# A banded attention and two MLPs in one planned kernel: the first MLP's tiles in blocks of 3, 4, 4, 4 and 3, a shorter warm-up and new priorities

## The chip, the cores and the metric

The kernel runs on one core of a Trainium2 chip. The metric is the device time of one execution in microseconds (us), given as the median of several runs.

## The reference

The input is q, k and v for 4 batches of 8 heads, 576 positions and 64 columns each. A causal attention within a window of 128 positions with a linear bias is followed by a first MLP with a rational activation and a second with SiLU; all is in float32.

```python
scores = scale * q @ k.T                      # per batch and head
scores = where((rel >= 0) & (rel < 128), scores - slope[h] * abs(rel), -1e9)
attn = softmax(scores); x = attn @ v          # -> x: 2304 tokens x 512
h = x @ w_in                                  # 512 x 2048
g = (a0 + a1*h + a2*h*h + a3*h**3) / (1 + |b0|*|h| + |b1|*h*h + 1e-6)
x = g @ w_out                                 # 2048 x 512
h = x @ w2_in;  g = h / (1 + exp(-h));  return g @ w2_out
```

The 2304 tokens are 18 tiles of 128.

## The kernel before

Every product of the MLPs is made of three products on numbers split into a high and a low part (xh and xl, gh and gl, and the two halves of a weight), so each has its elementwise work: a cast and a subtraction. The weights arrive as 64-bit numbers; ACT (L561, L564), DVE (L567), and ACT or POOL (L466, L474, L485) turn them into the two halves.

The first MLP works on blocks of tiles. `blk1` gives their sizes (4, 4, 3, 4 and 3). For each block and each of 16 slices f of the hidden layer, `step` issues 12 products into a bank `h` (L889 to L891; two banks in turn), a chain of five ACT and six DVE instructions for the rational function (L905 to L934), a cast and a subtraction that make gh and gl, and 12 products into four accumulators (L958 to L960). Each instruction works on the whole block at once, so on 512 columns for four tiles and 384 for three. Blocks 0 and 1 are taken in two parts each: f 0 to 9 of block 0, f 0 to 9 of block 1, then f 10 to 15 of both; partial sums go by way of DRAM. The first pass over a slice prepares its weights, and writes the first matrix's halves to a scratch (L597), from which later blocks read them (L606). Block 0 is therefore the one that pays for the weights.

Ahead of a block, `group` does its attention for four pairs of heads: scores (L698), masking and a minimum on DVE (L704, L711), the exponential on ACT (L715), the normalization on POOL (L734), a transposition (L754), masked copies (L785 to L803), the product with v (L831), and xh and xl (L846 to L855). Block 0's attention is done before its first step; block 1's beside block 0's f 0 to 9; block 2's only when block 0 is through, since x has two buffers.

The second MLP takes the 18 tiles in three groups of six by a scheme with seven products in place of eight. Sums of its weights are prepared on the way (`prep`, L1122) as filler work, written to DRAM, and streamed in (L1133).

The order of all this is made by a planner at build time. Each operation has a priority in units of steps, a cost, and one or more engines that may take it (for instance `'whi': 'act|pool'`); `schedule` simulates the engines and gives a free engine the ready operation of the best priority (`look` is how much later a better one may be). The constants in `OPT` and the list `SHIFTS` (first operation, count, shift) move priorities. The order that comes out is the order in each engine's queue; nothing is reordered on the chip. DMA issues nearly all lie in SP's queue. Before the first step, planned PE gaps of over 300 ns are filled with products on an identity whose result nobody uses (`spin`, L511): `warm` of them at the start, then `fill` (0.6) of each gap. A float32 product makes two records in the profile.

Of the kernel before, what the change touches and what calls it, by code (L numbers as in the profile page):

```python
# [30 lines left out]


OPT = {
    'blk1': '4,4,3,4,3',
    'res': 0,
    'lag': 2,
    'gh': 'act|pool',
# [13 lines left out]
    'tabs': 'pool',  # L51
    'stb': 3,
    'strb': 3,
    'wpro': 0.256,
    'dS': -1.52,
    'dT': 0.037,
    'dA': 0.149,
    'dm': 0.366,
    'look': 0.451,
    'pw': -0.72,  # L60
    'pwo': -0.374,
    'dg': -5.616,
    'lead': 2.536,
    'slk': 0,
    'warm': 6,
    'fill': 0.6,
    'fillmin': 300.0,
    'fs': 10,
    'ob': 3,
    'pl': -0.721,  # L70
    'vlead': -1.233,
    'qlead': -1.974,
    'keen': 9999.0,
    'norm0': 'pool',
    'sq': 'act',
# [4 lines left out]
    'mk02': 'dd',  # L80
    'mk03': 'dd',
    'xl00': 'd',
    'xl01': 'd',
    'xl02': 'p',
    'xl03': 'd',
    'alt': 0,
    'gh0': 'act|dve',
    'gl0': 'pool',
    'la': 8.921,
    'lb': 302.617,  # L90
    'dm2': 1.231,
    'sums': 'pool',
    'fhi': 'act|pool',
    'flo': 'dve|pool',
# [5 lines left out]
    'tsum': 'pool',  # L100
    'th': 'act|dve',
    'tl': 'dve|pool',
    'tlead': 1.016,
    'hlead': -0.505,
    'oq': 'sp',
    'pw2': 511.696,
    'rw2': 25.851,
    'pwo2': 1331.915,
    'rwo2': 14.569,
    'xlead': -0.854,  # L110
    'slead': 0.691,
    'shift': 'act',
    'tail': 1,
}
# [1 line left out]


SHIFTS = [
# [6 lines left out]
]  # L125


# [31 lines left out]
LAG = {"kd": 1400.0, "qd": 1400.0, "vh": 1400.0, "wraw": 1200.0, "ws": 400.0, "wv": 400.0, "tab": 0.0}  # L159
# [12 lines left out]
class Plan:  # L172
# [11 lines left out]
    def op(self, prio, eng, cost, fn, reads=(), writes=(), after=(), dma=False):  # L184

        o = Op()
        o.eng, o.cost, o.fn, o.prio, o.idx = eng, cost, fn, prio, len(self.ops)
        o.alts = eng if isinstance(eng, dict) else {eng: (cost, fn)}

        o.banks = {t[:2] for t in list(reads) + list(writes) if t[0] in ("h", "atA", "atB") or t[0].startswith("acc")}  # L190
        o.port = {e for e in o.alts if e == "pool" or e == "dve" and not o.banks}
        o.deps, o.allocs = set(after), []
        o.dma = dma or eng == "sp"
        o.lag = max([LAG.get(t[0], 0.0) for t in writes], default=0.0) if o.dma else 0.0
        for t in list(reads) + list(writes):
            key, reg = t[:2], t[2:]
            if key not in self.tile_ops:
                self.tile_ops[key] = []
                o.allocs.append(key)
            else:  # L200
                o.deps.add(self.tile_ops[key][0])
            self.tile_ops[key].append(o)
        for t in reads:
            key, reg = t[:2], t[2:]
            for w, r in self.writers.get(key, ()):
                if not reg or not r or r == reg:
                    o.deps.add(w)
        for t in writes:
            key, reg = t[:2], t[2:]
            for w, r in self.writers.get(key, ()):  # L210
                if not reg or not r or r == reg:
                    o.deps.add(w)
            for w, r in self.readers.get(key, ()):
                if not reg or not r or r == reg:
                    o.deps.add(w)
        for t in reads:
            self.readers.setdefault(t[:2], []).append((o, t[2:]))
        for t in writes:
            self.writers.setdefault(t[:2], []).append((o, t[2:]))
        o.deps.discard(o)  # L220
        self.ops.append(o)
        return o
# [166 lines left out]
def plan_kernel(ctx, tc, qn, kn, vp, table, w1, wo1, w2, wo2, out):  # L389
    nc = tc.nc if tc is not None else None  # L390
# [3 lines left out]
    RES, LAG = OPT["res"], OPT["lag"]  # L394
    pl = Plan()
# [64 lines left out]
    def do_copy(engs, n, make, psum=False, scale=None):  # L460

        sc = 1.0 if scale is None else scale

        def on_act():
            o, i = make()
            nc.scalar.activation(out=o, in_=i, func=AF.Copy, scale=sc) if scale is not None else nc.scalar.copy(o, i)  # L466

        def on_dve():
            o, i = make()
            nc.vector.tensor_scalar(out=o, in0=i, scalar1=sc, scalar2=None, op0=ALU.mult) if scale is not None else nc.vector.tensor_copy(o, i)  # L470

        def on_pool():
            o, i = make()
            nc.gpsimd.tensor_scalar(out=o, in0=i, scalar1=sc, scalar2=1.0, op0=ALU.mult, op1=ALU.mult)  # L474

        return any_of(engs, {"act": (c_act(n, psum), on_act), "dve": (c_dve(n) if psum else c_dve2x(n), on_dve), "pool": (c_pool_ts(n), on_pool)})

    def do_tt(engs, n, op, make):
        def on_dve():
            o, a, b = make()  # L480
            nc.vector.tensor_tensor(out=o, in0=a, in1=b, op=op)  # L481

        def on_pool():
            o, a, b = make()
            nc.gpsimd.tensor_tensor(out=o, in0=a, in1=b, op=op)  # L485

        return any_of(engs, {"dve": (c_dve(n), on_dve), "pool": (c_pool_tt(n), on_pool)})


    if tc is not None:  # L490
        nc.scalar.preload_act_table_set("natural_log_exp_and_others")
        tab_all = tab_p.tile([P, 6 * P + 16], F32, name="tab")
        tab = tab_all[:, :6 * P].rearrange("p (t c) -> p t c", c=P)
        coef = tab_all[:, 6 * P:]
        ident = const.tile([P, P], F32, name="ident")
# [18 lines left out]
        T[("h", "spin")] = h_p.tile([P, 512], F32, tag="h", name="spin")  # L514
        spin(OPT["warm"])

    pl.op(-98, "pe", 427 * OPT["warm"], first_spin, reads=[("ident", 0)], writes=[("h", "spin")])
    pl.spin = spin

    late = []  # L520

    def late_consts():
        for part, cols in ((0, slice(0, 3 * P)), (1, slice(3 * P, 6 * P + 16))):
            pl.op(-91.0 + 0.5 * part, "sp", 700, lambda cols=cols: nc.sync.dma_start(tab_all[:, cols], table[:, cols]), writes=[("tab", part)])
        for part in range(2):
            for h in range(H):
                pl.op(-70 + 0.1 * h + 10 * (h // 2) + 25 * part, do_copy("act" if h + part == 0 else OPT["tabs"], 2 * P,
                      lambda h=h, part=part: (tabs[:, h, 2 * part:2 * part + 2], tab[:, 4 * part:4 * part + 2]), scale=-8.0 * 2.0 ** -(h + 1)), 0, None,
                      reads=[("tab", part)], writes=[("tabs", h, part)])
        late.append(("na", 0))  # L530
        late.append(("ab", 0))
        pl.op(-3, "dve", 80, lambda: nc.vector.tensor_scalar(out=na, in0=coef[:, 0:4], scalar1=-1.0, scalar2=None, op0=ALU.mult),
              reads=[("tab", 1)], writes=[("na", 0)])
        pl.op(-3, "act", 200, lambda: nc.scalar.activation(out=ab, in_=coef[:, 4:6], func=AF.Abs), reads=[("tab", 1)], writes=[("ab", 0)])
# [457 lines left out]
    lead = OPT["lead"]  # L992
# [12 lines left out]

    att_load(0, -92, slot[0] + slot_w[0] - OPT["vlead"])
    late_consts()
    for gi in range(len(groups) - 1):
        att_load(gi + 1, slot[gi] - 0.25 * slot_w[gi] - OPT["qlead"], slot[gi + 1] + slot_w[gi + 1] - OPT["vlead"])
# [12 lines left out]
    for f in range(KF):  # L1022
        p = pos[0, f] + OPT["pw"]
# [4 lines left out]
        p = pos[0, f] + LAG + 0.5 + OPT["pwo"]  # L1028
# [431 lines left out]
```

## Time and profile before

| | |
|---|---|
| median of 3 runs | 869.03 us (868.75 to 869.29) |
| the profiled execution | 869.16 us; its span 867.3 us |
| PE busy | 855.2 us (99%), 5076 products |
| DVE, ACT, POOL busy | 643.1, 603.1, 637.9 us (74%, 70%, 74%) |
| granted TensorE clock | 1.00 in every stretch |
| DMA | 228.94 MB, 264 GB/s over the span |

The time of the profiled execution is 1.86 us longer than its span; the rest lies around the first and last instruction. PE's busy time counts the products on the identity too. The attention of block 0 and the first steps lie in the first 58 us, the rest of block 0's f 0 to 9 up to some 115 us, its f 10 to 15 near 175 to 200 us, and the second MLP from about 475 us to the end.

### The profile page before, as it was taken

Reading aid. Unit: us, or ns where it says so; the run is one execution under the profiler, and the core shown is the slowest. Engines: PE = TensorE matmul, PEld = TensorE weight load, DVE = VectorE, ACT = ScalarE, POOL = GpSimd, SP = SyncE. Lnnn points to the kernel's source line nnn. Section 1 sums busy time; section 2 is a strip of 40 time slices with the busy share of each in tenths; the row PEclk is TensorE's granted clock in tenths of the full one; section 3 lists DMA queues with packets and bytes.
Section 4 is the critical chain, followed back from the end, with each engine's and each line's share of the span. In section 5 each row is a group of like instructions: output and inputs, shape, how many; then the busy total and the mean of one; then the engine's idle time right before and its main releaser. Section 6 shows DMA issues by size and latency. Waiting matters only on the chain.

```text
span 867.3 us, 15300 instructions
## 1 busy us (share of the span) xinstructions
PE 855.2 (99%) x5076; PEld 765.1 (88%) x5076; DVE 643.1 (74%) x1308; ACT 603.1 (70%) x1291; POOL 637.9 (74%) x613
## 2 busy tenths in 40 slices
PE   8989999999999999999999999999999999999998
PEld 6667778877788998777889999999999999999998
DVE  7899897789999898998889984357733477433652
ACT  6699997799888988887889984446434365344452
POOL 4778845666888897878899677479954599744884
PEclk9999999999999999999999999999999999999999
DMA  7746764586889887876797889898888888878884
GB/s 253 264 161 214 243 223 137 169 277 227 289 310 321 294 280 263 306 255 238 275 349 240 295 297 356 262 318 281 281 277 250 292 288 282 295 248 258 252 269 169
DMA packets 80462, 228.94 MB, mean 264 GB/s; under 512 B 8192, under 2 KB 17152, under 8 KB 80384
## 3 DMA queue, kind: packets, MB, share of 16 engines
q1 hardware_dynamic: 78080, 219.59, 76.2%
q10 hardware_dynamic: 2304, 8.39, 2.4%
q8 instruction: 40, 0.66, 0.3%
q14 instruction: 38, 0.31, 0.1%
HBM read 178.66 MB, written 49.28 MB: 263 GB/s over the span
## 4 chain that ended last, share of the span: by engine, by line
PE 82%; DVE 5%; ACT 4%; POOL 3%; DMA 3%; issue 2%; SPq 0%; ACTq 0%; POOLq 0%; DVEq 0%
PE acc L958 6%; PE h L889 6%; PE acc L960 6%; PE acc L959 6%; PE h L891 5%; PE h L890 5%; PE z_a L1233 4%; PE z_b L1300 4%; PE z_a L1234 4%; PE z_a L1235 4%; PE z_b L1301 4%; PE z_b L1299 4%; PE bank_atA L831 3%; PE bank_atA L698 2%; PE bank_atA L1233 1%
## 5 line engine op out<-in xcount | busy, mean ns | idle before, releaser
L485 POOL TENSOR_TENSOR xl_b<-g,xh_b 128x384 fp32r<-128x384 f32 x81 | 90.6, 1119 | 69.6 <-ACT xh_b L466 67.8
L466 ACT CAST xh_b<-g 128x384 fp32r<-128x384 f32 x162 | 83.0, 514 | 64.3 <-PE z_b L1301 42.0
L958 PE MATMUL acc<-gh,wo 128*128 128x512 f32 (+1 forms) x320 | 121.1, 378 | 0.0
L960 PE MATMUL acc<-gl,wo 128*128 128x512 f32 (+1 forms) x320 | 118.7, 371 | 0.1
L959 PE MATMUL acc<-gh,wo 128*128 128x512 f32 (+1 forms) x320 | 117.8, 368 | 0.0
L481 DVE TENSOR_TENSOR xl_b<-g,xh_b 128x384 fp32r<-128x384 f32 x87 | 87.3, 1014 | 30.3 <-ACT xh_b L466 29.1
L485 POOL TENSOR_TENSOR gl<-t,gh 128x512 fp32r<-128x512 f32 (+1 forms) x76 | 93.0, 1224 | 15.9 <-ACT gh L466 12.5
L385 ACT ACTIVATE g<-t_a 128x384 f32<-128x384 f32 x72 | 37.9, 526 | 75.2 <-DVE t_a L378 75.2
L485 POOL TENSOR_TENSOR g<-g,g 128x384 f32<-128x384 f32 x72 | 84.5, 1185 | 2.0
L889 PE MATMUL h<-xh,ws 128*128 128x512 f32 (+1 forms) x224 | 84.2, 376 | 0.4 <-DVE t L934 0.4
L891 PE MATMUL h<-xh,ws 128*128 128x512 f32 (+1 forms) x224 | 82.2, 367 | 0.0
L890 PE MATMUL h<-xl,ws 128*128 128x512 f32 (+1 forms) x224 | 82.1, 367 | 0.0
L958 PEld LDWEIGHTS acc<-gh,wo 128*128 128x128 f32 x320 | 60.1, 188 | 13.4 <-issue 5.6
L960 PEld LDWEIGHTS acc<-gl,wo 128*128 128x128 f32 x320 | 60.0, 188 | 9.5 <-POOL gl L485 1.5
L959 PEld LDWEIGHTS acc<-gh,wo 128*128 128x128 f32 x320 | 60.1, 188 | 6.7
L1233 PE MATMUL z_a<-xf,w2s 128*128 128x384 f32 x192 | 64.2, 335 | 0.0
L1235 PE MATMUL z_a<-xf,w2s 128*128 128x384 f32 x192 | 64.1, 334 | 0.0
L1234 PE MATMUL z_a<-xf,w2s 128*128 128x384 f32 x192 | 64.1, 334 | 0.0
L1299 PE MATMUL z_b<-xh_b,wo2s 128*128 128x384 f32 x192 | 64.1, 334 | 0.0
L1300 PE MATMUL z_b<-xl_b,wo2s 128*128 128x384 f32 x192 | 64.1, 334 | 0.0
L1301 PE MATMUL z_b<-xh_b,wo2s 128*128 128x384 f32 x192 | 64.1, 334 | 0.0
L715 ACT ACTIVATE e<-e,m 128x128 f32<-128x128 f32 x144 | 56.0, 392 | 7.6 <-DVE m L711 7.3
(207 smaller groups left out, 2701.9 us busy)
## 6 DMA issues: line engine op xcount, KB each, us to landing
w2s<-forms_w SPq DMA_DIRECT2D x84, 512.0 KB, 4.7
wo2s<-forms_wo SPq DMA_DIRECT2D x84, 512.0 KB, 4.6
ws<-sc SPq DMA_DIRECT2D x64, 512.0 KB, 4.4
raw_w<-in_w SPq DMA_DIRECT2D x32, 512.0 KB, 4.9
raw_wo<-in_wo SPq DMA_DIRECT2D x32, 512.0 KB, 4.9
forms_w<-st_w SPq DMA_DIRECT2D x24, 512.0 KB, 5.0
forms_wo<-st_wo SPq DMA_DIRECT2D x24, 512.0 KB, 4.9
sc<-w ACTq DMA_DIRECT2D x16, 512.0 KB, 5.2
```

Of the source, the lines that this page charges most:

```text
L485: nc.gpsimd.tensor_tensor(out=o, in0=a, in1=b, op=op)
L889: nc.tensor.matmul(o, lhsT=T[W][:, 0, c], rhs=xh, start=kt == 0, stop=False)
L890: nc.tensor.matmul(o, lhsT=T[W][:, 0, c], rhs=xl, start=False, stop=False)
L891: nc.tensor.matmul(o, lhsT=T[W][:, 1, c], rhs=xh, start=False, stop=kt == KD - 1)
L958: nc.tensor.matmul(a, lhsT=T[WO][:, 0, c], rhs=T[G1][:, :n], start=first_f, stop=False)
L959: nc.tensor.matmul(a, lhsT=T[WO][:, 1, c], rhs=T[G1][:, :n], start=False, stop=False)
L960: nc.tensor.matmul(a, lhsT=T[WO][:, 0, c], rhs=T[G2][:, :n], start=False, stop=last_f)
L1233: nc.tensor.matmul(o, lhsT=w(0, kt * P), rhs=x[:, 0, kt], start=st and kt == 0, stop=False, skip_group_check=True)
L1234: nc.tensor.matmul(o, lhsT=w(0, kt * P), rhs=x[:, 1, kt], start=False, stop=False, skip_group_check=True)
L1235: nc.tensor.matmul(o, lhsT=w(1, kt * P), rhs=x[:, 0, kt], start=False, stop=kt == 1, skip_group_check=True)
L1299: nc.tensor.matmul(o, lhsT=w(0, m * P), rhs=h, start=st and q == 0, stop=False, skip_group_check=True)
L1300: nc.tensor.matmul(o, lhsT=w(0, m * P), rhs=l, start=False, stop=False, skip_group_check=True)
```

## The change

Block sizes become 3, 4, 4, 4 and 3: block 0 has 384 columns in place of 512, block 2 has 512 in place of 384. `warm` is 3 in place of 6. The subtraction that makes xl of the second pair of heads of block 0 goes from DVE to POOL (`xl01`), with a further copy on ACT (L848). In the planner, the loads of the first group are no longer given a delay after landing (tile numbers 0, up to 1400 ns), the two table loads cost 1150 in place of 700, and a warm-up product 470 in place of 427. Nearly all priority constants and all of `SHIFTS` have new values: among them the cast and subtraction of g (`dg`), the preparation of the second MLP's weights (`pw2`, `rw2`, `pwo2`, `rwo2`), its x (`xlead`) and streams (`slead`), and the planned length of its second half (`lb`, which spaces its priorities).

```diff
-    'blk1': '4,4,3,4,3',
+    'blk1': '3,4,4,4,3',
...
-    'wpro': 0.256,
-    'dS': -1.52,
...
-    'look': 0.451,
...
-    'dg': -5.616,
-    'lead': 2.536,
-    'warm': 6,
+    'wpro': 0.378,
+    'dS': -1.535,
...
+    'look': 0.3,
...
+    'dg': -1.9,
+    'lead': 2.673,
+    'warm': 3,
...
-    'xl01': 'd',
+    'xl01': 'p',
...
-    'la': 8.921,
-    'lb': 302.617,
+    'la': 9.168,
+    'lb': 28.335,
...
-    'pw2': 511.696,
-    'rw2': 25.851,
-    'pwo2': 1331.915,
-    'rwo2': 14.569,
-    'xlead': -0.854,
-    'slead': 0.691,
+    'pw2': 104.137,
+    'rw2': 39.941,
+    'pwo2': 483.456,
+    'rwo2': 34.48,
+    'xlead': -2.659,
+    'slead': -0.54,
...
 SHIFTS = [
-    (47, 4, -0.61), (257, 3, 0.14), (291, 1, 1.63), (341, 4, 0.79), ...
+    (283, 4, -0.5), (297, 19, 0.39), (438, 2, 2.39), (554, 53, -0.59), ...
...
-        o.lag = max([LAG.get(t[0], 0.0) for t in writes], default=0.0) if o.dma else 0.0
+        o.lag = max([LAG.get(t[0], 0.0) for t in writes if t[1] != 0], default=0.0) if o.dma else 0.0
...
-    pl.op(-98, "pe", 427 * OPT["warm"], first_spin, ...
+    pl.op(-98, "pe", 470 * OPT["warm"], first_spin, ...
...
-            pl.op(-91.0 + 0.5 * part, "sp", 700, ...
+            pl.op(-91.0 + 0.5 * part, "sp", 1150, ...
```

## Rows read from the trace of the kernel before

**Rows 1.** Stretches: length, busy us of PE, PEld, DVE, ACT, POOL, clock, DMA.
```profile
0.00:6.00 6.00, 4.64 (x28) 4.19 (x28) 3.00 (x8) 1.70 (x2) 2.18 (x10) 1.00 0.61 165
6.00:42.00 36.00, 33.13 (x339) 23.66 (x332) 30.76 (x142) 26.04 (x100) 25.34 (x32) 1.00 0.77 271
42.00:58.00 16.00, 13.14 (x95) 9.56 (x94) 14.27 (x34) 14.43 (x36) 10.25 (x10) 1.00 0.62 207
58.00:115.00 57.00, 57.00 (x343) 43.44 (x342) 52.90 (x124) 54.76 (x121) 47.00 (x40) 1.00 0.62 205
...
175.00:200.00 25.00, 23.82 (x114) 18.79 (x113) 21.16 (x43) 23.00 (x44) 17.36 (x16) 1.00 0.78 262
...
475.00:867.00 392.00, 388.88 (x2235) 386.74 (x2233) 218.68 (x316) 195.19 (x387) 272.88 (x241) 1.00 0.84 276
```

**Rows 2.** Line 511 alone: PE's products on the identity, durations in ns.
```profile
L511 PE MATMUL spin<-ident x62: 275/275/582, 1.4 to 27.3; 128*128 128x128 f32 x62
...
L511 PE MATMUL bank_acc<-ident x38: 272/275/377, 30.7 to 53.2; 128*128 128x128 f32 x38
```

**Rows 3.** PE's instructions in order of time, first 6 us: start, us, what, wait.
```profile
1.36 3.78 PE L511 MATMUL spin<-ident 128*128 128x128 f32 x16 [1.36 <-POOL ident masks.py:199]
5.07 0.57 PE L698 MATMUL bank_atA<-kd,qd 64*128 64x128 f32 x1
```

**Rows 4.** SP's, ACT's and DVE's instructions in the first 7 us.
```profile
1.17 0.42 SPq L636 DMA_DIRECT2D qd<-in_qn  x1
...
4.47 0.42 ACT L466 ACTIVATE tabs<-tab 128x256 f32<-128x256 f32 x1 [2.46 <-DMA tab<-in_table]
...
6.30 0.29 DVE L704 COPY_PREDICATED bank_atA<-tab,bank_atA 128x128 f32<-128x128 uint32 x1 [2.11 <-PE bank_atB L698]
```

**Rows 5.** DMA issues of the first 50 us: KB each, median us to landing.
```profile
qd<-in_qn SPq DMA_DIRECT2D x2, 128.0 KB, 2.6
```

**Rows 6.** ACT's and PE's instructions in order of time, 41 to 55 us.
```profile
41.09 0.69 ACT L561 ACTIVATE raw_w<-raw_w 128x512 f32<-128x512 f32 x1 [3.35 <-DMA raw_w<-in_w]
...
47.03 1.95 PE L511 MATMUL bank_acc<-ident 128*128 128x128 f32 x16
...
52.13 1.38 PE L511 MATMUL bank_acc<-ident 128*128 128x128 f32 x10
54.52 0.50 PE L889 MATMUL h<-xh,w 128*128 128x512 f32 x1 [1.01 <-DVE t L934]
```

**Rows 7.** PE's products of 512 columns in order of time, at 32 us.
```profile
31.75 0.39 PE L890 MATMUL h<-xl,w 128*128 128x512 f32 x1
31.98 0.39 PE L891 MATMUL h<-xh,w 128*128 128x512 f32 x1
```

**Rows 8.** Groups by shape, DVE and ACT, 58 to 475 us: busy us, mean ns.
```profile
L932 DVE SCALAR_TENSOR_TENSOR h<-t,na,h 128x512 f32<-128x512 f32 x46 | 34.4, 749 | 0.0
L930 DVE SCALAR_TENSOR_TENSOR t<-t,h 128x512 f32<-128x512 f32 x46 | 31.5, 685 | 15.6 <-ACT h L928 15.5
L932 DVE SCALAR_TENSOR_TENSOR h<-t,na,h 128x384 f32<-128x384 f32 x20 | 12.3, 616 | 0.0
L930 DVE SCALAR_TENSOR_TENSOR t<-t,h 128x384 f32<-128x384 f32 x20 | 11.0, 550 | 4.0 <-ACT h L928 4.0
...
L911 ACT ACTIVATE t<-h,na 128x512 f32<-128x512 f32 x46 | 35.5, 773 | 0.0
L911 ACT ACTIVATE t<-h,na 128x384 f32<-128x384 f32 x20 | 13.3, 664 | 0.0
```

**Rows 9.** The same for POOL: the subtraction that makes gl, both shapes.
```profile
L485 POOL TENSOR_TENSOR gl<-t,gh 128x512 fp32r<-128x512 f32 x47 | 62.3, 1325 | 11.3 <-ACT gh L466 8.4 <-DVE gh L470 2.0
...
L485 POOL TENSOR_TENSOR gl<-t,gh 128x384 fp32r<-128x384 f32 x18 | 18.3, 1019 | 0.6 <-ACT gh L466 0.3
```

**Rows 10.** PE's instructions in order of time, at 188 us.
```profile
188.04 0.50 PE L889 MATMUL h<-xh,w 128*128 128x512 f32 x1 [1.18 <-DVE t L934]
```

**Rows 11.** The page's DMA issues: KB each, median us to landing.
```profile
w2s<-forms_w SPq DMA_DIRECT2D x84, 512.0 KB, 4.7
```

More of the change, by code (lines that the diff above doesn't have):

```diff
@@ L53 @@
     'strb': 3,
-    'wpro': 0.256,
-    'dS': -1.52,
-    'dT': 0.037,
-    'dA': 0.149,
-    'dm': 0.366,
-    'look': 0.451,
-    'pw': -0.72,
-    'pwo': -0.374,
-    'dg': -5.616,
-    'lead': 2.536,
+    'wpro': 0.378,
+    'dS': -1.535,
+    'dT': -0.058,
+    'dA': 0.258,
+    'dm': 0.356,
+    'look': 0.3,
+    'pw': -0.815,
+    'pwo': -0.633,
+    'dg': -1.9,
+    'lead': 2.673,
     'slk': 0,
-    'warm': 6,
+    'warm': 3,
     'fill': 0.6,
@@ L69 @@
     'ob': 3,
-    'pl': -0.721,
-    'vlead': -1.233,
-    'qlead': -1.974,
+    'pl': 0.738,
+    'vlead': -1.491,
+    'qlead': -2.527,
     'keen': 9999.0,
@@ L88 @@
     'gl0': 'pool',
-    'la': 8.921,
-    'lb': 302.617,
-    'dm2': 1.231,
+    'la': 9.168,
+    'lb': 28.335,
+    'dm2': -0.436,
     'sums': 'pool',
@@ L102 @@
     'tl': 'dve|pool',
-    'tlead': 1.016,
-    'hlead': -0.505,
+    'tlead': 0.0,
+    'hlead': -1.106,
     'oq': 'sp',
-    'pw2': 511.696,
-    'rw2': 25.851,
-    'pwo2': 1331.915,
-    'rwo2': 14.569,
-    'xlead': -0.854,
-    'slead': 0.691,
+    'pw2': 104.137,
[4 more added lines that the diff above has]
+    'slead': -0.54,
     'shift': 'act',
@@ L515, in first_spin @@
         spin(OPT["warm"])
-    pl.op(-98, "pe", 427 * OPT["warm"], first_spin, reads=[("ident", 0)], writes=[("h", "spin")])
+    pl.op(-98, "pe", 470 * OPT["warm"], first_spin, reads=[("ident", 0)], writes=[("h", "spin")])
     pl.spin = spin
@@ L523, in late_consts @@
         for part, cols in ((0, slice(0, 3 * P)), (1, slice(3 * P, 6 * P + 16))):
-            pl.op(-91.0 + 0.5 * part, "sp", 700, lambda cols=cols: nc.sync.dma_start(tab_all[:, cols], table[:, cols]), writes=[("tab", part)])
+            pl.op(-91.0 + 0.5 * part, "sp", 1150, lambda cols=cols: nc.sync.dma_start(tab_all[:, cols], table[:, cols]), writes=[("tab", part)])
         for part in range(2):
```

12 rows, old and new, of the table SHIFTS are left out of this document.

## The prediction

> **What bounds the kernel now.** I read the table of stretches first. From 58 us on PE is busy nearly all the time, and in the second MLP 2235 products take 388.88 us, 0.174 us each, at a granted clock of 1.00 [rows 1]. Products of 512 columns start 0.23 us apart (31.75, 31.98) [rows 7]. So behind 58 us the kernel is bound by PE, whose work the change leaves the same: every tile still meets every weight once. What can be won lies in PE time that does no useful work. The busy share hides it, since line 511 counts as work: 100 records on the identity [rows 2]. The first 16 take 3.78 us [rows 3] and 16 later ones 1.95 us, 0.122 each [rows 6].
>
> So I split the start. Up to 6 us: nearly all lost but the first scores. From 6 to 42 us, the attention of block 0: PE idles 36 - 33.13 = 2.9 us [rows 1], and of the 100 records 100 - 16 - 16 - 10 = 58 lie in it [rows 2, 3, 6], 58 x 0.122 = 7.1 us; 10.0 us are lost. From 42 to 58 us: 2.9 idle and 26 x 0.122 = 3.2 on the identity, 6.0 lost [rows 1, 6]. Behind that some 1.2 us at 175 to 200 us [rows 1, 10]. That is about 20 us in all, and a gain of more than 10 is out of reach for an edit that leaves most of the start as it is.
>
> **The head: fewer warm-up products.** qd, the last of what the first scores need, is issued at 1.17 and lands 2.6 us later [rows 4, 5], so they could start at 3.8. They start at 5.07, behind 16 records that end at 5.1 [rows 3]: 1.3 us too late. DVE's first real work at 6.30 waited for them, while its table was there at 4.47 [rows 4]. With at most four products, eight records of 3.78 / 16 = 0.236 us, PE is free at 1.36 + 1.9 = 3.3, before the data. DVE then starts at about 5.3 in place of 6.3, if the twelve records of the first scores are somewhat slower than now. I take -0.9; ends -1.3 and 0, the latter if the next loads set the pace.
>
> The granted clock reads 1.00 here too [rows 1], yet the first 16 records cost twice what later ones do (0.236 against 0.122): by this PE ran at the lower of its two levels, 1.2 GHz, before it reached 2.4 GHz, and had done nothing but these products. The Trainium skill, "TensorE: Matmul & The Clock Gate", section "What's actually happening", says that the slow state is the default and that activity lifts it; by that, fewer warm-up products leave the first scores at the slow level, and the head's gain shrinks. What this would cost here is worked out from the rows under the second rival.
>
> **Block 0's attention, three tiles for four.** Per pair of heads the number of instructions that work on a half of the block stays, those of a tile fall by a quarter. If what is lost in 6 to 42 us shrinks with the tiles, a quarter of 10.0 is -2.5. Ends: -3.5, if the smaller loads also shorten ACT's wait of 3.35 us for raw weights [rows 6], and 0, if that wait and the weights, which do not shrink, set the length. I take -2.5, since DVE with 30.76 of 36 us is nearest to the bound [rows 1] and its work there is mostly attention. The useful work taken out returns in block 1 and is no gain.
>
> **The first steps.** At 47.03 and 52.13 PE runs on the identity; the next h waits at 54.52 for the last operation of a step's chain [rows 6]. The chain is six DVE operations (three like L932, three like L930, each within 10 ns) and five on ACT: DVE 3 x (749 + 685) = 4.30 us at 512 columns and 3 x (616 + 550) = 3.50 at 384; L911 falls by 109 ns, and five such by 0.55 [rows 8]. The chain is 1.35 us shorter. I take -1.2 of the 6.0 us lost; ends -2.0 (both waits shrink) and 0 (weights come late).
>
> **The rest of block 0's f 0 to 9.** This speaks against the change. At 58 to 115 us PE is full, but ACT has 54.76 of 57 us and DVE 52.90 [rows 1]. A step at 384 columns saves PE 24 x (0.23 - 0.174) = 1.34 us, DVE 0.80, ACT 0.55 + 0.11 for the cast = 0.66, POOL 1.325 - 1.019 = 0.31 [rows 1, 7 to 9]; the weights and block 1's attention don't shrink. Over nine steps: PE needs 57 - 12.1 = 44.9, ACT 54.8 - 5.9 = 48.9, DVE 52.9 - 7.2 = 45.7, POOL 47.0 - 2.8 = 44.2. If ACT keeps its share, at the 96% that it reaches now, the stretch takes 50.9 and PE loses 6.0. If the planner shares casts out evenly (whi may go to ACT or POOL), each of the three has 46.3 and PE loses 1.4. I take +1.4, since POOL has ten free microseconds here and the planner gives an operation to the engine that is free first; ends 0 and +6.0.
>
> **Block 0's f 10 to 15.** PE waits there for the same chain, 1.18 us [rows 10], with ACT at 23.00 of 25 [rows 1]. Six steps: PE -8.0, ACT -4.0, DVE -4.8. ACT and PE would then need 19.0 and 15.8; up to 3.2 us lost against 1.2 now, less what is prepared ahead in block 1's part. I take +0.5; ends -1.2 and +2.0.
>
> **Edits costed at nothing.** xl of the second pair: DVE loses a subtraction like L930 (0.68), ACT gains a copy and POOL a subtraction like L485's 1.33 [rows 8, 9], at a place where POOL has 10.7 of 36 us free [rows 1]; if its later end were waited for, up to +0.7. Block 2 at 512 columns has more PE work per fixed elementwise cost: 0. The second MLP's new priorities: covered by DVE, ACT and POOL that are busy for 219, 195 and 273 of 392 us [rows 1]; without that cover one late stream costs up to its 4.7 us to landing [rows 11]. SP's queue is moved past new neighbours throughout; whatever waits there holds all loads behind it. SHIFTS, look, dg and the leads have no row of their own: between -1.2 (the stall at 188 us goes) and +2.0 (a few new waits of that size); 0, as PE hardly waits there now.
>
> **Sum.** -0.9 - 2.5 - 1.2 + 1.4 + 0.5 = -2.7. On the profiled execution's 869.16 (its span 867.3 and 1.86 around it) that is 866.46; the median lies 0.13 lower, so 866.3.
>
> **The rivals.**
> 1. Slower: block 0 is starved. Narrow steps with the whole weight work make ACT the bound up to 115 us and again at 175 us: +6.0 and +2.0 in place of +1.4 and +0.5, 866.3 + 6.1 = 872.4. For it: ACT's 96%. Against: POOL's idle ten. The gain of 4.6 from the start is used up when the two stretches lose 4.6: with 0.5 in the second, when the first takes 44.9 + 4.1 = 49.0 us, that is when ACT keeps more than 0.96 x 49.0 = 47.0 us of work in it.
> 2. The same: PE stays slow. The eight records that are gone are replaced by eight of real work at the slow pace, 8 x (0.236 - 0.122) = 0.9, and a pause before the data prolongs it by, say, another 16, 1.8: 869.0. For it: the pace of the first 16. Against: PE is not the bound of the first 6 us.
> 3. The same: the shorter blocks don't shorten the start, because raw weights do (ACT's 3.35 us). Without -2.5 and -1.2: 870.0.
> 4. Much faster: all terms at their low ends, -1.3 - 3.5 - 2.0 + 0 - 1.2 = -8.0: 861.0. It needs an order without new waits.
>
> **How the numbers follow.** A measurement of this kernel can tell about 0.2%, 1.7 us. My forecast has 0.46 (own range 864 to 868.5; 0.38 of it faster, 0.08 the same); rival 1 0.23 (0.03 the same, as its mild form, 0.20 slower); rival 2 0.10 and rival 3 0.08 (together 0.12 the same, 0.06 slower); rival 4 0.13. Faster 0.51, same 0.23, slower 0.26. The range reaches to the main part of rivals 1 and 4: 861.5 to 872.5.
>
> **What would show it.** Head: the first scores near 3.8 us and DVE's first masking near 5.3. Attention: the first h products some 5 us earlier than now, at 32 us [rows 7], fewer than 80 records of line 511. Block 0: PE's busy share in the stretch up to block 1's first steps; below 92% with ACT above 95% is rival 1. Wrong altogether would be PE idle behind 200 us, above all in the second MLP, which I costed at nothing.

## The result, and the profile after

The changed kernel takes 882.04 us (881.82 to 882.97, 4 runs), the kernel before beside it 868.89 (868.63 to 869.29): a ratio of 1.0149, 95% interval 1.0135 to 1.0163. It is 13 us slower, where 866.3 was predicted, in a range of 861.5 to 872.5.

The stretches of the profile after, in the columns and at the places of [rows 1]; the last one begins at 475 us, as there, and ends with the span of 880.3 us. PE's first product of the second MLP (L1233) comes behind that, at 507.4 us before and at 512.5 us here, so the row holds the end of the first MLP too:

```profile
0.00:6.00 6.00, 4.64 (x24) 3.61 (x25) 3.87 (x13) 1.78 (x3) 2.24 (x11) 1.00 0.57 159
6.00:42.00 36.00, 34.19 (x308) 25.55 (x306) 28.71 (x137) 27.94 (x105) 26.86 (x35) 1.00 0.77 265
42.00:58.00 16.00, 12.85 (x102) 10.09 (x102) 14.92 (x44) 15.39 (x40) 12.18 (x12) 1.00 0.68 237
58.00:115.00 57.00, 53.87 (x361) 45.40 (x360) 51.11 (x119) 53.19 (x116) 40.55 (x36) 0.97 0.69 245
175.00:200.00 25.00, 23.60 (x154) 20.07 (x154) 20.08 (x54) 23.70 (x56) 16.40 (x16) 1.00 0.89 297
475.00:880.00 405.00, 398.31 (x2286) 397.30 (x2285) 224.01 (x329) 202.78 (x392) 273.60 (x245) 1.00 0.82 268
```

The fourth row is the one to see: from 58 to 115 us PE had no idle time before and has 3.1 us now, and its granted clock is 0.97 in place of 1.00. The last row has 6.7 us of idle time where before had 3.1 in 392.

To add up where the 13 us are, the busy share doesn't help, as the prediction said. So I took, at the first product of a step, the time less what all useful PE instructions before it take at full pace, by their usual distance from start to start in the traces: 0.1735 us for a product of 384 columns, 0.2265 for 512, 0.0535, 0.0945 and 0.1065 for a score, a product with v and a transposition. What is left is time lost to waits, to the slow clock and to the identity. Steps count in the order of the queue (0 to 9 are block 0's f 0 to 9, 10 to 19 block 1's, 20 to 25 block 0's f 10 to 15, 32 to 47 block 2).

| stretch | lost before, us | lost after | difference | predicted |
|---|---|---|---|---|
| start to step 3 | 27.98 | 27.11 | -0.87 | -4.6 |
| steps 3 to 9 | 1.94 | 7.78 | +5.84 | +1.4 |
| steps 10 to 19 | 1.01 | 1.07 | +0.06 | 0 |
| steps 20 to 25 | 2.38 | 2.73 | +0.35 | +0.5 |
| steps 26 to 63 | 7.17 | 10.95 | +3.78 | 0 |
| step 64 to the first MLP's last product (the seam) | 2.04 | 5.89 | +3.85 | 0 |
| the rest of the second MLP | -0.32 | -0.33 | -0.01 | 0 |

The sum is +13.0. Kernels with the same order in a stretch still differ there, by up to 1.3 us in steps 3 to 9 and 1.8 in steps 26 to 63 (10.95 here, 9.14 in a_silu_last below), so less than that is not read from single profiles. At the seam the ten kernels with this order lose 5.9 to 8.9 us, and the row above is the lowest of them. Three places need an explanation first: the missing gain at the start, block 0, and the seam; the 3.8 us of steps 26 to 63 come up again at the end.

**The start.** PE's first instructions after, then DVE's first masking (start, us, what, wait), and line 511's records:

```profile
1.36 2.07 PE L511 MATMUL spin<-ident 128*128 128x128 f32 x8 [1.36 <-POOL ident masks.py:199]
3.44 0.55 PE L698 MATMUL bank_atA<-kd,qd 64*128 64x128 f32 x1
...
5.01 2.07 PE L511 MATMUL spin<-ident 128*128 128x128 f32 x8
```
```profile
5.13 0.30 DVE L704 COPY_PREDICATED bank_atA<-tab,bank_atA 128x128 f32<-128x128 uint32 x1 [0.94 <-PE bank_atB L698]
```
```profile
L511 PE MATMUL spin<-ident x60: 275/275/581, 1.4 to 27.4; 128*128 128x128 f32 x60
...
L511 PE MATMUL bank_acc<-ident x26: 275/275/377, 34.9 to 45.9; 128*128 128x128 f32 x26
```

The head did what was predicted: scores at 3.44 (5.07 before, [rows 3]), masking at 5.13 (6.30, [rows 4]). Of the 1.6 us that the scores come earlier the masking keeps 1.2: the slow pace of the second rival is there (the eight identity records at 5.01 take 2.07 us like the first eight). But the first product into h starts at 30.5 us against 31.4, 0.9 earlier and not 5, and line 511 still has 86 records. By then 18.6 us are lost, against 18.2 before: h comes earlier only because 1.3 us less useful work stands ahead of it.

**Block 0.** The chain that ended last, from 64 to 80 us (start, us, what):

```profile
64.03 1.33 POOL w L485
65.36 0.02 issue
65.38 4.76 DMA raw_wo<-in_wo
...
70.16 0.69 ACT raw_wo L561
70.84 1.41 ACT e L715 x7
...
72.29 0.68 ACT raw_wo L564
...
73.01 1.02 POOL gl L485
74.03 1.71 POOL ph L790
...
75.82 1.63 POOL ph L792
...
77.49 2.95 PE bank_atA L831 x20
```

PE's instructions around it, and the stretch behind:

```profile
75.20 0.34 PE L891 MATMUL h<-xh,w 128*128 128x384 f32 x1
77.49 2.09 PE L831 MATMUL bank_atA<-ph,vh 128*64 128x256 f32 x14 [1.96 <-POOL ph L792]
```
```profile
78.30:81.70 3.40, 3.40 (x20) 2.44 (x17) 3.29 (x4) 3.30 (x8) 3.40 (x4) 0.50 0.01 1
```

A raw weight is loaded only when POOL's subtraction has freed its buffer (65.36), and lands at 70.14. ACT, idle for 0.48 us until then, takes it ahead of seven instructions of the exponential; DVE's cast that makes gh follows them, and then gl and the two maskings of block 1's attention on POOL. This chain is one of several: DVE had no idle time of over 0.3 us between 66 and 78 us. PE, which now needs a quarter less time per step, stands there for 1.96 us (2.1 from start to start), and then runs for 3.4 us at a granted clock of 0.50, its lower level of 1.2 GHz, which costs up to 1.7 us more. These two are 3.8 of the 5.8 us. In all PE is idle for 4.4 us in steps 3 to 9; before, it was not idle in them at all.

**The seam.** ACT's instructions from 520 us on, PE's, DVE's wait between them, and the stretch behind:

```profile
520.33 1.28 ACT L385 ACT_TABLE_LOAD   x1
521.62 0.49 ACT L385 ACTIVATE g<-z_a 128x384 f32<-128x384 f32 x1
522.13 1.28 ACT L926 ACT_TABLE_LOAD   x1
523.42 0.62 ACT L926 ACTIVATE t<-t,lnb 128x384 f32<-128x384 f32 x1
...
524.46 1.28 ACT L928 ACT_TABLE_LOAD   x1
525.76 0.58 ACT L928 ACTIVATE bank_atB<-t,lnb 128x384 f32<-128x384 f32 x1
...
526.90 1.28 ACT L385 ACT_TABLE_LOAD   x1
528.19 0.52 ACT L385 ACTIVATE g<-t_a 128x384 f32<-128x384 f32 x1
```
```profile
524.84 0.34 PE L960 MATMUL acc<-gl,wo 128*128 128x384 f32 x1
528.90 0.69 PE L1233 MATMUL bank_atA<-xf,w2s 128*128 128x384 f32 x1 [3.72 <-DVE t_a L378]
```
```profile
526.37 0.55 DVE L930 SCALAR_TENSOR_TENSOR t<-t,bank_atB 128x384 f32<-128x384 f32 x1 [4.70 <-ACT bank_atB L928]
```
```profile
528.85:532.25 3.40, 3.35 (x10) 3.35 (x11) 1.68 (x2) 1.13 (x3) 3.23 (x4) 0.50 0.92 298
```

The second MLP's first SiLU (L385) now stands in ACT's queue ahead of the last logarithm (L926) and exponential (L928) of the rational function. They need different function tables, so ACT loads four tables, 5.1 us, in eight. Up to here one load, at 0.73 us, had served both logarithm and exponential (the kernel asks for that table at L491); behind the SiLU each of the two gets a load of its own. Before, the order had one load here, behind the last exponential:

```profile
512.28 0.58 ACT L928 ACTIVATE bank_atB<-t,lnb 128x384 f32<-128x384 f32 x1
...
513.46 1.28 ACT L385 ACT_TABLE_LOAD   x1
```

DVE waits 4.70 us for L928, and PE for DVE: 3.72 us idle, and again 3.4 us at 0.50 behind it. The Trainium skill, "ScalarE: Activation LUTs", section "What ACT_TABLE_LOAD costs", gives about 1283 ns for the load, as these rows do, and some 1380 ns for a drain with every switch; of the latter nothing shows here, since the load at 522.13 starts where the SiLU ends (521.62 + 0.49).

### The profile page after: what moved, and what is told of

It is laid out like the page before. It is cut to its first block, busy times and chain, and to the rows that moved or that the text cites. A ratio compares the mean times of both kernels' runs of the same rounds, so it can differ in the third digit from the quotient of the medians.

```text
span 880.3 us, 15286 instructions
## 1 busy us (share of the span) xinstructions
PE 860.5 (98%) x5062; PEld 767.5 (87%) x5062; DVE 645.2 (73%) x1313; ACT 610.4 (69%) x1297; POOL 628.3 (71%) x606
## 4 chain that ended last, share of the span: by engine, by line
PE 77%; DVE 8%; POOL 4%; ACT 4%; DMA 4%; issue 3%; POOLq 0%; SPq 0%; ACTq 0%; DVEq 0%
PE h L889 5%; PE acc L958 5%; PE acc L959 5%; PE acc L960 5%; PE h L891 5%; PE h L890 5%; PE z_b L1301 4%; PE z_b L1299 4%; PE z_b L1300 4%; PE z_a L1235 4%; PE z_a L1233 4%; PE z_a L1234 4%; PE bank_atA L831 3%; PE bank_atA L698 2%; PE bank_atB L1233 1%
## 5 line engine op out<-in xcount | busy, mean ns | idle before, releaser
L960 PE MATMUL acc<-gl,wo 128*128 128x512 f32 (+1 forms) x320 | 118.5, 370 | 0.0
L485 POOL TENSOR_TENSOR gl<-t,gh 128x512 fp32r<-128x512 f32 (+1 forms) x72 | 88.8, 1234 | 16.8 <-ACT gh L466 12.5
L385 ACT ACTIVATE g<-t_a 128x384 f32<-128x384 f32 x72 | 37.8, 526 | 76.9 <-DVE t_a L378 76.8
L889 PE MATMUL h<-xh,ws 128*128 128x512 f32 (+1 forms) x224 | 87.7, 391 | 0.7 <-DVE t L934 0.6
L891 PE MATMUL h<-xh,ws 128*128 128x512 f32 (+1 forms) x224 | 85.7, 382 | 0.0
L890 PE MATMUL h<-xl,ws 128*128 128x512 f32 (+1 forms) x224 | 85.7, 382 | 0.0
L960 PEld LDWEIGHTS acc<-gl,wo 128*128 128x128 f32 x320 | 60.4, 189 | 8.2 <-POOL gl L485 0.4
L1233 PE MATMUL z_a<-xf,w2s 128*128 128x384 f32 x192 | 64.1, 334 | 0.0
```

Of the source, the lines that this page charges most:

```text
L889: nc.tensor.matmul(o, lhsT=T[W][:, 0, c], rhs=xh, start=kt == 0, stop=False)
L890: nc.tensor.matmul(o, lhsT=T[W][:, 0, c], rhs=xl, start=False, stop=False)
L891: nc.tensor.matmul(o, lhsT=T[W][:, 1, c], rhs=xh, start=False, stop=kt == KD - 1)
L960: nc.tensor.matmul(a, lhsT=T[WO][:, 0, c], rhs=T[G2][:, :n], start=False, stop=last_f)
L1233: nc.tensor.matmul(o, lhsT=w(0, kt * P), rhs=x[:, 0, kt], start=st and kt == 0, stop=False, skip_group_check=True)
```

## The experiments

Kernels named a_ are the kernel after with one edit, b_ the kernel before with one edit, c_ either kernel without `SHIFTS`. Where nothing else is said the order of all queues stays that of the kernel it was made from; in the c_ kernels, a_silu_last and a_seam_mask the planner makes a new one. Times are medians; ratios are to the kernel before on the same chip, whose median lay between 868.89 and 869.93 on the chips used, so that two medians compared across chips can be off by 1 us. Each profile is of one execution.

**The seam: SiLU behind the last exponential (a_silu_last).**

```diff
+        exps.append(pl.ops[-1])        # behind L928
...
+                if g == 0 and j in (2, 4, 5, 6):
+                    pl.ops[-1].deps |= set(exps)   # the first group's SiLUs wait for all L928
```

> The changed kernel, with one edit: the first SiLUs of the second MLP wait for the last exponential of the first. The order is the changed kernel's up to 508 us; some 45 places differ behind it. Theory: the order mixes two kinds of ACT function at the seam, so ACT loads its table four times from 520 to 528 us (1.28 us each), PE stands for 3.72 us and then runs 3.4 us at half its clock; with one load left the kernel is 4 to 5.5 us faster than the changed one, about 877. Rival: the last steps of the first MLP are late anyway and PE waits for them instead; then less than 1 us is won.

875.99 us, ratio 1.0065 (1.0040 to 1.0089), 6.0 us less than after (7.3 by the two ratios). ACT at that place:

```profile
519.60 0.62 ACT L928 ACTIVATE t<-t,lnb 128x384 f32<-128x384 f32 x1
...
520.85 1.28 ACT L385 ACT_TABLE_LOAD   x1
522.15 0.49 ACT L385 ACTIVATE g<-z_a 128x384 f32<-128x384 f32 x1
```

One load is left, PE has no wait of over 0.4 us from 515 us on, and from step 64 to the first MLP's end 0.9 us are lost in place of 5.9. So the order that makes the tables alternate is the seam's loss, and some 5 to 7 of the 13 us. It is also what the Trainium skill's rule says ("ScalarE: Activation LUTs", section "Table sets: the hidden batching unit"): batch calls by table set. The planner's cost for an ACT instruction has no term for the load, so nothing kept its order from this.

**The head (a_warm8: eight warm-up products in the kernel after; b_head: two in the kernel before).**

```diff
-        spin(OPT["warm"])
+        spin(8)      # a_warm8; spin(2) in b_head
```

> The changed kernel in its own order, with eight warm-up products in place of three (and one of filling), so that the first scores start near 5.1 us again in place of 3.4. Theory that the head's time is on the path: 0.8 to 1.6 us slower than the changed kernel. Rival: loads and DVE set the pace of the first 20 us anyway: within 0.3 us.

> The kernel before in its own order, with two warm-up products in place of six (and two of filling), so that the first scores start near 4 us in place of 5.1. If the head's time were on the path: 0.8 to 1.2 us faster than the kernel before. By the run with eight in the changed kernel, which lost nothing at the first h product: within 0.4 us of the kernel before.

a_warm8: 883.08, 1.0141 (1.0114 to 1.0168). Its first scores come at 5.50 us, 2.1 later than in after, and its first product into h at 30.2 against 30.5. b_head: 868.93, 1.0002 (0.9991 to 1.0013); scores at 3.47 in place of 5.07, first h at 31.2 in place of 31.4. a_warm8's time alone can't tell (1.0 us above after by the medians, 0.7 below by the ratios), but in both runs what comes earlier at 5 us has waited again by 30 us: the head is worth nothing that can be measured.

**The split and the constants apart (five kernels without SHIFTS).** `SHIFTS` moves operations by their number, so it fits one split only; without it, split and constants can be exchanged.

```diff
-SHIFTS = [ ... ]
+SHIFTS = [ ]
-    'blk1': '4,4,3,4,3',
+    'blk1': '3,4,4,4,3',     # c_before_new; c_after_old the reverse; c_before_4344: '4,3,4,4,3'
```

> The kernel before, with the list SHIFTS empty: blocks 4, 4, 3, 4, 3 and the old constants. One of four kernels without SHIFTS, which were found for one split each. Both theories: some us slower than with SHIFTS, 872 to 880; it is the first corner.

> The kernel before with the blocks 3, 4, 4, 4, 3 alone, no SHIFTS. Theory that the split starves block 0: 4 to 9 us slower than the same with the old split. Theory that only the new constants are bad: within 2 us of it.

> The changed kernel with SHIFTS empty: blocks 3, 4, 4, 4, 3 and the new constants. Theory that the split starves block 0: 4 to 9 us slower than the next, and its loss lies between 58 and 118 us. Theory that only the constants are bad: within 2 us of the next.

> The changed kernel's constants with the old blocks 4, 4, 3, 4, 3, no SHIFTS. Theory of the split: 4 to 9 us faster than the one ahead. Theory of the constants: 4 us or more slower than the first corner and within 2 us of the one ahead. Whether ACT's table ping-pong at the seam is there (loads of 1.28 us) is read from the trace: if it is there with the new constants and either split, it comes from the constants.

> The kernel before without SHIFTS and with the blocks 4, 3, 4, 4, 3: the narrow block comes second, where no weights are prepared in its first part. Theory that a narrow block 0 starves because all weights fall into it: the time lost by PE between the step numbers 3 and 10 is that of the old split without SHIFTS (3.3 us), not that of 3, 4, 4, 4, 3 (12.7), and the whole lies at 880 to 884. Rival: any narrow block among the first two, or any split other than the old, fits the old constants badly: lost 7 us or more there, 885 to 889.

| without SHIFTS | blocks | us | ratio | first h at | lost to step 3 | steps 3 to 9 | from step 64 to the first MLP's end |
|---|---|---|---|---|---|---|---|
| c_before_old | 4,4,3,4,3 | 880.32 | 1.0127 | 31.6 | 27.3 | 3.3 | 3.9 |
| c_before_new | 3,4,4,4,3 | 888.29 | 1.0211 | 26.6 | 28.7 | 12.7 | 1.7 |
| c_after_new | 3,4,4,4,3 | 886.00 | 1.0195 | 30.2 | 25.6 | 9.3 | 6.2 |
| c_after_old | 4,4,3,4,3 | 889.36 | 1.0238 | 31.4 | 32.9 | 3.6 | 6.0 |
| c_before_4344 | 4,3,4,4,3 | 888.02 | 1.0208 | 31.8 | 29.7 | 3.0 | 5.1 |

Several things follow. The narrow block 0 loses 9 to 13 us in steps 3 to 9 with either set of constants, the wide one 3 to 4: this loss belongs to the split. c_before_new's stretch shows it without the other changes:

```profile
58.00:115.00 57.00, 51.01 (x334) 43.94 (x323) 48.21 (x113) 48.55 (x111) 40.66 (x36) 0.91 0.63 210
```

By the whole time, though, the split costs 8.0 us with before's constants only. With after's the wide block was expected 4 to 9 us faster and is not (889.36 against 886.00): it loses 7.3 us more ahead of step 3, and that eats up what it saves behind.

The four table loads stand in both kernels with after's constants, and one load in the three with before's: the four belong to the constants. The prediction's "first h 5 us earlier" is there, in c_before_new (26.6 against 31.6; 1.9 us of it are less time lost, the rest is work that comes later), and is given back by step 3, where 1.4 us more are lost than with the wide block. And the lists themselves matter as much as the rest: `SHIFTS` is worth 10.8 us to the kernel before (880.32 against 869.49 on the same chip) and 4.0 to the one after. Without a list the two kernels are 5.7 us apart and not 13. A split of 4, 3, 4, 4, 3 keeps block 0's steps whole as expected, but loses 4.4 us in the next ten steps (block 1, narrow there), where c_before_old loses 1.5; its total, 888.02, lies where the rival put it (885 to 889) and not at the 880 to 884 that I had expected.

**What holds PE in block 0: less work on one engine.** ACT's scaling of the low words left out (a_act_less); POOL's subtraction made a copy of half the time (a_pool_less); both (a_both_less); DVE's joining of the words cut to 64 columns (a_dve_less); all three (a_all_less). Each for the first MLP's weights.

```diff
# ACT, L564: the instruction is not issued for w1 and wo1
-    lambda: nc.scalar.activation(out=low(), in_=low(), func=AF.Copy, scale=LOW_SCALE)
+    lambda: nc.scalar.activation(...) if name[-1] == "2" else None
...                              # L567 then takes its second operand from top() in place of low()
# POOL, L485 for weights
-    do_tt(lo_eng, NR, ALU.subtract, lambda: (T[wk][:, 1, :], raw_view(T[rk]), T[wk][:, 0, :].bitcast(F32)))
+    nc.gpsimd.tensor_scalar(out=T[wk][:, 1, :], in0=raw_view(T[rk]), scalar1=1.0, scalar2=1.0, ...)
# DVE, L567
-    out=top().bitcast(U32), in0=top().bitcast(U32), ...
+    out=top()[:, :64].bitcast(U32), in0=top()[:, :64].bitcast(U32), ...
```

> The changed kernel in its own order, with ACT's second weight instruction (line 564, 0.67 us) left out for the first MLP's 32 weights; the weights are not the true ones. Theory that ACT bounds block 0: the 13 us that ACT sheds there take the stalls at 75 and 95 to 99 us away, 4 to 6 us faster than the changed kernel, about 877. Theory that the weights' own pipeline (three raw buffers, landing to POOL) sets the pace: also faster, but by the share that this instruction has in a weight's 10 us, 1 to 3 us. Theory that only the order is bad: less than 1 us.

> The changed kernel in its own order, with POOL's subtraction for the low half of the first MLP's weights (1.32 us) replaced by a copy of half its length; the low halves are not the true ones. Theory that ACT bounds block 0: nothing, within 1 us of 882. Theory that the weights' pipeline sets the pace: as much as the ACT variant, 1 to 3 us faster, since both take 0.67 us from each weight. Theory that POOL's queue is what PE waits for at 75 us: 4 to 6 us faster.

> The changed kernel in its own order, with both edits of the two runs before: ACT's line 564 left out and POOL's subtraction replaced by a copy of half its length, for the first MLP's weights, which are not the true ones. Theory that ACT, DVE and POOL share the bound in block 0, so that relief of one moves the wait to the next: both together win more than the sum of the two alone (1.8 + 1.1): 4 to 7 us, 876 to 878. Theory that the waits come from the order alone: the sum or less, 879 to 881.

> The changed kernel in its own order, with DVE's weight instruction (line 567) working on 64 of 512 columns for the first MLP's 32 weights; the weights are not the true ones. ACT at 83% and POOL at 61 to 63% of the stretch won nothing in the runs before, while DVE stayed at 92 to 93%. Theory that DVE is what starves PE in block 0: it sheds some 0.6 us per weight, 12 us between 20 and 110 us; PE's lost time between the step numbers 3 and 10 falls from 7.8 us to under 4, and the kernel takes 876 to 878. Rival, that raw weights land late (three buffers, 4.8 us each) and the chain of single waits in the queues' order sets the pace: 6 to 8 us stay lost, 880 to 882.

> The kernel after with the weight work of the first MLP made shorter on three engines at once, each as in its own run: ACT's scaling of the low words (L564) left out, POOL's subtraction replaced by a copy of half its time, DVE's joining of the words (L567) on 64 of 512 columns. Order kept; the output is not the reference's. If several chains that end almost together hold PE in block 0: lost in steps 3 to 10, which was 7.8 us in after and 6.5, 9.2, 7.0 and 8.9 with ACT, POOL, ACT and POOL, and DVE relieved, falls under 4.5 us, the product with v near 75 us waits less than 0.7 us, and the kernel comes to 876 to 878. If PE's own queue order sets it, whatever the engines do: lost stays above 6 us and the kernel within 1.5 us of 879.7, what ACT and POOL together gave.

| | us | ratio (interval) | lost in steps 3 to 9 | PE's wait near 75 us |
|---|---|---|---|---|
| after | 882.04 | 1.0149 (1.0135 to 1.0163) | 7.8 | 1.96 |
| a_act_less | 880.28 | 1.0119 (1.0090 to 1.0148) | 6.5 | 1.95 |
| a_pool_less | 880.93 | 1.0122 (1.0096 to 1.0147) | 9.2 | 1.98 |
| a_both_less | 879.71 | 1.0120 (1.0106 to 1.0135) | 7.0 | 1.97 |
| a_dve_less | 879.40 | 1.0111 (1.0072 to 1.0149) | 8.9 | 1.17 |
| a_all_less | 876.75 | 1.0080 (1.0059 to 1.0101) | 5.8 | 1.17 |

The last column is the wait of the product with v for the mask, as in the row shown of after. The stretch of these steps in after, a_both_less, a_dve_less and a_all_less (columns of [rows 1]):

```profile
55.50:103.00 47.50, 44.33 (x304) 37.78 (x305) 42.97 (x99) 43.48 (x94) 35.72 (x30) 0.96 0.64 228
```
```profile
54.90:101.60 46.70, 44.03 (x304) 37.96 (x305) 43.53 (x99) 38.84 (x83) 29.44 (x30) 0.96 0.65 235
```
```profile
55.00:103.60 48.60, 43.49 (x305) 36.48 (x305) 37.79 (x99) 42.72 (x93) 33.45 (x30) 1.00 0.63 218
```
```profile
53.70:99.20 45.50, 42.97 (x305) 36.75 (x306) 38.65 (x99) 38.05 (x83) 26.83 (x30) 1.00 0.66 232
```

In after no engine is full (PE 93%, ACT 92%, DVE 90%, POOL 75%). In a_both_less ACT has 4.6 us less to do and POOL 6.3, the stretch is 0.8 us shorter, and the wait for the mask is the same. So neither "ACT is the bound" nor "POOL is" holds. With DVE relieved that wait does shrink, by 0.8 us, but five other waits of 0.5 to 1.2 us take its place between 78 and 97 us, and the stretch is no shorter. (This profile's execution took 883.54 us where the median is 879.40, so its extra 1.1 us say nothing.) Only a_all_less's interval lies clear of after's. It is 5.3 us faster, as I had expected if several chains end close together (876 to 878); but the wait for the mask is 1.17, where I had expected under 0.7, and the loss in these steps fell only to 5.8, where I had expected under 4.5. PE's idle time in them fell even less, from 4.4 to 3.8 us; the clock, at 1.00 in place of 0.96, can give up to 1.7 us, which covers the rest. The gain beyond that lies in steps 10 to 63 (11.6 us lost in place of 14.8, but a_silu_last with no engine relieved has 13.0 there) and ahead of step 3. So the total bears the theory out and the steps it was about do not.

**What holds PE in block 0: single waits taken away.** a_no_mask2 leaves out L792 for block 1; a_wo_ready gives block 0's f 0 to 9 the halves of the first slice of the second matrix, which are ready; a_mask_wo does both.

```diff
# a_no_mask2, a_mask_wo (L791)
-    lambda ...: nc.gpsimd.tensor_tensor(out=prev_(), in0=prev_(), in1=own_(), op=ALU.subtract)
+    lambda ...: None if bi == 1 else nc.gpsimd.tensor_tensor(out=prev_(), ...)
# a_wo_ready, a_mask_wo (L879, L958 to L960)
+        WO_ = wkey[("wo1", 0, 0)] if blk == 0 and f < FS else WO
-            nc.tensor.matmul(a, lhsT=T[WO][:, 0, c], ...)
+            nc.tensor.matmul(a, lhsT=T[WO_][:, 0, c], ...)
```

> The kernel after, with the second masking subtraction on POOL (L792) left out for block 1's attention (four operations of some 1.3 to 1.6 us); the order of every queue is kept, and the output is not the reference's. If one stall makes most of the loss (the product with v at 75 us waits 1.96 us for this operation, the stretch behind it ran at a granted clock of 0.50 for 3.4 us): the wait at 75 us shrinks by 1.6 us to under 0.7, the dip of the clock behind it goes, and PE's time lost in steps 3 to 10 falls from 7.8 to about 4.3 us; whole kernel -3 to -4 us, 878 to 879. If weights late at many steps make it: the waits come back at the next products, lost stays above 6.5 us, whole kernel -0 to -1.3.

> The kernel after, but in block 0's f 0 to 9 the products into the accumulators read the halves of the first slice of the second matrix, which are ready long before, in place of their own; every operation that prepares the weights stays, and so does the order. The output is not the reference's. If weights that come late hold PE: lost in steps 3 to 10 falls from 7.8 to under 5 us, whole kernel -3 us or more. If PE waits for the masks and the chain of the rational function: lost stays within 1 us of 7.8, the wait at 75 us is still there, whole kernel within 1.5 us of after.

> The kernel after with L792 left out for block 1's attention, and block 0's f 0 to 9 products into the accumulators on the first slice's weight halves, which are ready. Order kept; the output is not the reference's. Each alone left lost at 8.3 and 8.4 us. If the two waits only stood behind each other: the product with v comes at 76.2 in after's time (1.3 earlier), no wait of 1.4 for the weight follows, the granted clock does not fall, lost in steps 3 to 10 is 4 to 5 us, and the kernel 878 to 879.5. If a third chain (masks and xl on DVE) stands as close behind: lost above 6.5 us, kernel above 880.

a_no_mask2: 882.65, 1.0137 (1.0107 to 1.0166), 8.1 us lost in steps 3 to 9. PE there:

```profile
76.19 1.95 PE L831 MATMUL bank_atA<-ph,vh 128*64 128x256 f32 x20 [0.37 <-POOL ph L790]
78.07 0.44 PE L958 MATMUL acc<-gh,wo 128*128 128x384 f32 x1
79.92 0.44 PE L959 MATMUL acc<-gh,wo 128*128 128x384 f32 x1 [1.41 <-POOL wo L485]
```

a_wo_ready: 881.29, 1.0136 (1.0119 to 1.0152), 8.4 lost; the product with v waits 2.0 us for the mask, up to 76.3 us, as it does in after. a_mask_wo: 883.91, 1.0173 (1.0143 to 1.0204), 7.8 lost. PE there (L961 is after's L960), and its stretch:

```profile
79.00 0.34 PE L961 MATMUL acc<-gl,wo 128*128 128x384 f32 x1
81.97 0.41 PE L754 MATMUL bank_atA<-ident,e 128*128 128x128 f32 x2 [2.64 <-DVE xl L855]
```
```profile
55.80:103.30 47.50, 42.94 (x305) 36.69 (x306) 40.94 (x99) 43.22 (x94) 31.72 (x27) 1.00 0.61 216
```

This is the clearest reading of the study: with the mask gone PE waits for a weight, with the weight ready it waits for the mask, with both gone for xl on DVE, and each time the same 8 us are lost. Mask and weight are POOL's, xl is DVE's. So the steps are not paced by one instruction; several chains through these queues stand about equally far behind PE.

**Two effects together (a_seam_mask: a_silu_last and a_no_mask2).**

> The kernel after with both edits: the first group's SiLU operations wait for the last exponential of the rational function (one load of a function table in place of four at the seam of the MLPs), and L792 left out for block 1's attention. If the two losses are apart and add: 882.0 - 6.0 - 3.5 = 872.5, range 871 to 874. If the stall in block 0 is not L792: 876, as with the first edit alone.

875.19, 1.0064 (1.0041 to 1.0087), against 875.99 for the seam's edit alone: the second case of the expectation, and once more that the mask alone is worth nothing that can be measured.

## Why the prediction was wrong

- **Head, -0.9.** Its mechanism was right to 0.4 us at 3.44 and 5.13 us; its worth was not. The step that failed is that what PE and DVE gain at 5 us reaches the end. By the first h of a_warm8, and by b_head's time, it is worth nothing. The end 0 was in the range, for the reason named there (the next loads).
- **Block 0's attention, -2.5, and the first steps, -1.2.** Up to step 1 (42 us before) the lost time fell by 0.8 us, where with the head 3.4 were predicted; by step 2 it had fallen by 2.7, by step 3 by 0.9 only. The step that failed is the scaling of the loss with the tiles. The chain of a step did get shorter, but the wait for its last operation did not: 1.24 us at step 3 here, 1.01 before [rows 6]:

```profile
55.54 0.44 PE L889 MATMUL h<-xh,w 128*128 128x384 f32 x1 [1.24 <-DVE t L934]
```

  With before's constants the first h did come 5 us earlier, and that was lost again. Rival 3 said that the weights, which don't shrink, would stand in the way. In after, POOL's queue just before the first h fits this, with a weight's cast and subtraction ahead of the last normalization before it (L734), for which PE waits 0.7 us; that the weights made the rest of the missing gain is not shown:

```profile
25.25 0.66 POOL L474 TENSOR_SCALAR w<-raw_w 128x512 fp32r<-128x512 f32 x1 [0.71 <-DVE l L726]
25.98 1.30 POOL L485 TENSOR_TENSOR w<-raw_w,w 128x512 fp32r<-128x512 f32 x1
27.24 1.62 POOL L734 TENSOR_TENSOR e<-e,l 128x512 f32<-128x512 f32 x2
```

- **The rest of block 0's f 0 to 9, +1.4.** This is the term of the sum that failed most: +5.8, nearly the +6.0 of the first rival. That the rival's price came out is luck, since its mechanism was not there: it asked for ACT above 95% and PE below 92%, and these steps have 92% and 93% (43.48 and 44.33 of 47.50 us). What the runs show in its place is 4.4 us of single waits, for chains that end at about the same time, and up to 1.7 us of slow clock, for which neither had a term. My reason against it, POOL's ten idle microseconds, was a fault of method: I divided the work of three engines as if it could be poured from one to the other, but each instruction stands at a fixed place in a queue behind others that wait, and PE meets the last of several chains. Idle time in sum is not idle time where it is needed. c_before_new shows the same loss without the new constants.
- **f 10 to 15 of block 0, +0.5.** +0.35; right within what can be read.
- **xl of the second pair, block 2, SHIFTS and look, 0 each.** From step 26 to 63 3.8 us more are lost, 2.0 by a_silu_last, which has the same order there. Three waits of 0.5 to 1.1 us (at 206, 217 and 331 us) make 2.2 of the 3.8, where before had one of 0.6; of the three a_silu_last has only that at 217. The rest is spread in smaller ones. The prediction allowed up to +2.0 for "a few new waits of that size". Without a list before loses more in these steps than after (13.4 against 11.5, c_before_old and c_after_new), and its list takes 6.3 us out of them, after's list 0.6: the step that failed is to take the exchange of the two lists as worth nothing. That SHIFTS was worth 10.8 us to the kernel before I had no row for: a list of shifts that removes waits leaves no trace of the waits that it removed.
- **The second MLP's new priorities, 0.** Behind the seam that was right: -0.01. At the seam it was not, +3.85 in that table and 5 to 7 us by a_silu_last. I looked for what a late stream could cost, and not at what a changed order costs on an engine whose instructions have a price that depends on their neighbours. That PE idle behind 200 us would show the prediction "wrong altogether" was the right test, and it came true at 525 us.

What stays open: which of the new priorities puts SiLU ahead of the last exponential, and how far more buffers for raw weights (there are three) would have helped block 0, which was not tried. Nor is it settled why 5.8 us stay lost in steps 3 to 9 with all three engines relieved; the order of the queues is what remains, but no run reordered them alone. None of these kernels is faster than the one before.

## What to carry to other kernels

Where PE has just enough cover, cutting its work per step while each step's other work stays can be a loss in these steps, even if every other engine has idle time in sum: look for how many chains end within a microsecond of PE's next instruction, and expect that taking away one wait only shows the next. Before moving priorities across the border of two phases, list which function tables ACT needs on both sides, and check that the order changes them once; a planner without a cost for the load can mix them. A tuned list of shifts is bound to its split and constants: change one and cost the list's loss too, by a run of the kernel without it.

## What the runs showed of the hardware

- Behind two waits of PE (1.96 us at 75 us, 3.72 us at 525 us) its granted clock stood at 0.50 for 3.4 us, which cost up to 1.7 us each time. But a_act_less's wait of 1.95 us at the same place and a_mask_wo's of 2.64 us at 79 us brought no fall (1.00 over steps 3 to 9 in both), so the length of the wait alone did not decide it here. Nor did it decide for how long: a_act_less has the same 3.72 us at the seam, and its clock stood at 0.50 from 523.1 to 529.9 us.
- A load of a function table took 1.28 us in each of the six cases shown. In the row of four loads ACT's next instruction starts within 0.02 us of each load's end.
- Cutting DVE's joining of the words from 512 to 64 columns took 5.2 us off DVE in steps 3 to 9 (42.97 to 37.79), and these steps took 48.6 us in place of 47.5. The 1.1 us are within what single profiles differ by, but nothing of the 5.2 us shows in the length of the steps.
